# PSUM as three double and two single banks from the second batch on: a second product on two banks, attention in four pieces, double-bank relus

## The chip, the cores and the metric

One core of a Trainium2 chip runs the whole kernel. The metric is device time in microseconds (us) of one execution, as a median over runs. All runs compared here are with a granted TensorE clock of 0.999 or 1.000.

Engines are named as the profile names them: PE is TensorE, PEld its weight loads, DVE VectorE, ACT ScalarE, POOL GpSimd, SP the engine that issues stores and transposing transfers. The kernel uses PSUM, the memory that PE writes its results to, as eight banks of 128 x 512 fp32.

## The reference, cut to what matters

```python
# q, k, v: (8, 8, 1024, 64); E, F: (64, 1024); w_in: (512, 2048); w_out: (2048, 512)
k_proj = np.einsum('ks,bhsd->bhkd', E, k)
v_proj = np.einsum('ks,bhsd->bhkd', F, v)
scores = np.matmul(q, k_proj.transpose(0, 1, 3, 2)) / 8
attn = softmax(scores)                       # over the 64 projected keys
x = np.matmul(attn, v_proj) -> (8192, 512)   # heads side by side
h = np.maximum(x @ w_in, 0.0)                # first product
out = h * h @ w_out                          # second product
```

## The kernel before: the parts that matter

The kernel works batch by batch (b = 0 to 7). While PE computes the two dense products of batch b, small pieces of attention for batch b+1 are slipped in between. A batch is two chunks of 512 tokens. A chunk's first product runs in eight pairs of blocks (k = 0 to 7), each block four matmuls into one PSUM bank; ACT takes the relu out of the bank, DVE squares the pair, and from k = 4 on DVE also forms operand sums. The second product is then computed from these sums in seven products (p1 to p7 in the code) of 16 matmuls each, into 128 x 512 outputs x, y, z; one matmul fills half a bank. Where a product is cut, a and b or lo and hi are its parts.

```python
    aps = ctx.enter_context(tc.tile_pool(name="aps", bufs=2, space=bass.MemoryType.PSUM))  # 2 double banks
    fps = ctx.enter_context(tc.tile_pool(name="fps", bufs=4, space=bass.MemoryType.PSUM))  # 4 single banks
    ...
    PIECES = {       # attention of the next batch, by step of the current one (batches 2 to 6)
        1: "copy_kp", 2: "copy_vp", 4: "copy_v_down",
        20: "scores 0, scores 1, exponentials 0", 21: "exponentials 1",
        23: "sums 0, values 0 0, reciprocals 0", 25: "normalize 0 0",
        28: "scores 2, scores 3, exponentials 2", 29: "exponentials 3",
        47: "values 0 1, sums 1, reciprocals 1", 48: "normalize 0 1",
        53: "values 1 0, values 1 1", 54: "normalize 1 0", 55: "normalize 1 1",
    }
    ...
            def square(k, n, ps):                  # n: first or second block of pair k
                ...
                    nc.scalar.activation(r[:, n], ps[:], AF.Relu)
                ...                                # after n == 1: DVE squares r, then operand sums
            def step1(k, n):
                ...
                ps = ffn_psum("ps_h")              # one single bank
                first(ch, HFB * h + j, ps, range(NCB))
                square(k, n, ps)
    ...
            def p1a():                             # steps of the second product
                st["x"], st["y"], st["z"] = (bank(n) for n in ("ps_x", "ps_y", "ps_z"))
                ...
                product(st["y"], st["A11"], W11, lo, True)
            def p2a(): ...                         # x: first half of A12 * W21
            def p1b(): ...                         # y: A11 * W11, needs DVE's squares up to k = 6
            def p1c(): ...                         # y: its last two matmuls, need the square of k = 7; ACT copies y
            def p2b():
                product(st["x"], st["A12"], W21, hi)
                add(st["o0"][:, :, 0:MH], "x", st["a"])   # DVE
            ...
            second = [p1a, p2a, p1b, p1c] + lohi(p5) + lohi(p6) + lohi(p3) + lohi(p7) + [p2b]
            second += [p4_last] if last else lohi(p4)
```

Steps count through a batch: 0 to 15 the first product of the first chunk, 16 to 30 its second product, 31 to 46 and 47 to 61 the same for the second chunk. `scores`, `sums` and `values` are groups of small matmuls that use the array in several tiles at once.

The softmax here doesn't subtract the row's maximum and nothing guards it: scores larger than these inputs give would overflow.

## Time and profile before

| | kernel before |
|---|---|
| time, median of three runs | 484.09 us (483.77 to 484.11) |
| span of the profiled run | 482.4 us |
| first matmul of batch 1 | at 82.33 us |
| a steady batch (2 to 5) | 57.30 us |
| batch 6; first matmul of batch 7 to the end | 55.46; 55.8 us |

PE's share, its waits and the stretches by batch are shown in the prediction below. Beside them, two lines of the page's costliest groups: line, engine, operation, output and input, count, then busy us, mean ns of one, and idle time before.

```profile
L521 DVE TENSOR_TENSOR hsq<-h_relu 128x1024 bf16<-128x1024 f32 x123 | 149.9, 1222 | 75.0 <-ACT h_relu L513 74.2
L513 ACT ACTIVATE h_relu<-ps_h 128x512 f32<-128x512 f32 x255 | 149.4, 597 | 63.4 <-PE ps_h L459 63.0
```

These are the squares and the relus.

### The profile page before, as it was taken

How to read it: one execution, taken by the hardware profiler on the slowest of the kernel's cores; microseconds unless marked ns; L12 is line 12 of the kernel's file. 1: busy time of each engine (PE TensorE's matmuls, PEld its weight loads, DVE VectorE, ACT ScalarE, POOL GpSimd, SP SyncE). 2: the span in 40 equal slices, each digit the busy share in tenths (PEclk: the TensorE clock that was granted, in tenths of full speed). 3: DMA queues.
4: the chain of work that ended last, by engine and by line, in shares of the span. 5: the costliest groups of instructions: out<-in, count | busy, mean ns of one | idle time of the engine just before them, and what ended most of it. 6: DMA issues, size and time to landing. Idle time of an engine off the chain costs nothing.

```text
span 482.4 us, 8423 instructions
## 1 busy us (share of the span) xinstructions
PE 470.3 (97%) x3630; PEld 292.6 (61%) x3630; DVE 314.1 (65%) x382; ACT 261.5 (54%) x413; POOL 34.7 (7%) x48
## 2 busy tenths in 40 slices
PE   4899999999999999999999999999999999999997
PEld 2544676475574746657475665747557474666656
DVE  1478955554958559493776848667494855948383
ACT  2387544758427564466635667176662756545351
POOL 6540020020020001000010000100000000000000
PEclk9999999999999999999999999999999999999999
DMA  9999989579989086941859147690702102020202
GB/s 155 203 204 207 168 181 200 137 120 229 180 128 229 12 175 88 180 94 50 153 86 227 22 115 131 91 200 1 165 11 75 25 1 88 1 88 0 88 1 87
DMA packets 72789, 55.46 MB, mean 115 GB/s; under 512 B 33968, under 2 KB 64944, under 8 KB 72752
## 3 DMA queue, kind: packets, MB, share of 16 engines
q0 software_dynamic: 30624, 29.36, 39.4%
q1 hardware_dynamic: 42128, 25.56, 21.1%
q8 instruction: 28, 0.46, 0.4%
q14 instruction: 9, 0.07, 0.0%
HBM read 59.24 MB, written 16.78 MB: 158 GB/s over the span
## 4 chain that ended last, share of the span: by engine, by line
PE 92%; DVE 3%; DMA 3%; ACT 1%; POOL 1%; issue 0%; POOLq 0%
PE ps_h L459 44%; PE ps_y L479 23%; PE ps_z L479 11%; PE ps_x L479 6%; DMA V_sb<-in_v_dram 3%; PE ps_kv L180 2%; PE ps_att L221 2%; PE ps_att L206 2%; DVE hsq L521 1%; DVE s L473 1%; PE ps_v L284 0%; DVE xT L246 0%; DVE xT L351 0%; PE ps_kv L181 0%; ACT h_relu L513 0%; POOL K_sb L93 0%
## 5 line engine op out<-in xcount | busy, mean ns | idle before, releaser
L459 PE MATMUL ps_h<-xT,w_in 128*128 128x512 bf16 x1024 | 224.8, 379 | 0.2 <-DVE xT L351 0.2
L521 DVE TENSOR_TENSOR hsq<-h_relu 128x1024 bf16<-128x1024 f32 x123 | 149.9, 1222 | 75.0 <-ACT h_relu L513 74.2
L513 ACT ACTIVATE h_relu<-ps_h 128x512 f32<-128x512 f32 x255 | 149.4, 597 | 63.4 <-PE ps_h L459 63.0
L459 PEld LDWEIGHTS <-w_in 128*128 128x128 bf16 x1024 | 99.7, 98 | 117.7 <-issue 1.9
L479 PEld LDWEIGHTS <-s 128*128 128x128 bf16 x1024 | 98.5, 98 | 19.8 <-issue 8.7
L479 PEld LDWEIGHTS <-hsq 128*128 128x128 bf16 x768 | 73.8, 98 | 17.3 <-issue 3.8
L479 PE MATMUL ps_y<-T,s 128*128 128x256 bf16 x512 | 62.4, 273 | 0.0
L246 DVE TENSOR_TENSOR xT<-ps_att,rs 128x1024 bf16<-128x1024 f32 x28 | 33.4, 1215 | 17.6 <-ACT rs L236 17.0
L473 DVE TENSOR_TENSOR s<-hsq 128x1024 bf16<-128x1024 bf16 x64 | 43.5, 683 | 0.0
L591 ACT COPY o_sb<-ps_y 128x512 f32<-128x512 f32 x15 | 8.8, 586 | 53.8 <-PE ps_y L479 53.7
L213 ACT ACTIVATE expT<-ps_att 128x1024 bf16<-128x1024 f32 x28 | 27.2, 1025 | 14.0 <-PE ps_att L206 14.0
L479 PE MATMUL ps_x<-w_out,hsq 128*128 128x256 bf16 x256 | 33.2, 273 | 0.0
L479 PE MATMUL ps_y<-w_out,hsq 128*128 128x256 bf16 x256 | 33.2, 273 | 0.0
L595 DVE TENSOR_TENSOR o_sb<-ps_z,p_b 128x512 f32<-128x512 f32 x16 | 11.0, 688 | 33.8 <-issue 19.9
L479 PE MATMUL ps_y<-T,hsq 128*128 128x256 bf16 x256 | 30.9, 272 | 0.0
L479 PE MATMUL ps_z<-T,s 128*128 128x256 bf16 x256 | 30.6, 273 | 0.0
L479 PE MATMUL ps_z<-w_out,s 128*128 128x256 bf16 x256 | 30.6, 273 | 0.0
L591 ACT COPY p_b<-ps_y 128x512 f32<-128x512 f32 (+1 forms) x17 | 9.4, 556 | 25.9 <-PE ps_y L479 25.8
L81 POOL DMA_DIRECT2D Q_sb<-in_q_dram x7 | 6.1, 876 | 227.7 <-DMA qT<-Q_sb 227.2
L473 DVE TENSOR_TENSOR s<-s,hsq 128x1024 bf16<-128x1024 bf16 x32 | 21.8, 684 | 0.3
L473 DVE TENSOR_TENSOR s<-hsq,s 128x1024 bf16<-128x1024 bf16 x32 | 21.7, 682 | 0.0
L591 ACT COPY p_a<-ps_y 128x512 f32<-128x512 f32 (+1 forms) x17 | 9.4, 561 | 21.8 <-PE ps_y L479 21.6
(75 smaller groups left out, 233.0 us busy)
## 6 DMA issues: line engine op xcount, KB each, us to landing
out_dram<-o_sb SPq DMA_DIRECT2D x30, 512.0 KB, 3.8
K_sb<-in_k_dram POOLq DMA_DIRECT2D x7, 1024.0 KB, 15.3
V_sb<-in_v_dram POOLq DMA_DIRECT2D x7, 1024.0 KB, 22.4
Q_sb<-in_q_dram POOLq DMA_DIRECT2D x7, 1024.0 KB, 9.4
w_out<-in_moe_w_out_dram POOLq DMA_DIRECT2D x4, 512.0 KB, 13.2
w_in<-in_moe_w_in_dram POOLq DMA_DIRECT2D x7, 256.0 KB, 10.0
K_sb<-in_k_dram POOLq DMA_DIRECT2D x2, 512.0 KB, 8.5
out_dram<-o_sb SPq DMA_DIRECT2D x3, 256.0 KB, 2.1
```

The lines of the kernel that those rows point to most:

```text
L180: nc.tensor.matmul(ps[0:KP, :], lhsT=ET[:, i, :], rhs=kv[:, :, i, :], start=f, stop=l)
L206: nc.tensor.matmul(ps[o, bank, :], lhsT=self.kT[r, 2 * pr + j, :], start=True, stop=True, rhs=self.qT[r, NT * (2 * pr + j):NT * (2 * pr + ...
L213: nc.scalar.activation(e[:], self.ps["s", pr][:], AF.Exp, scale=SCALE)
L221: nc.tensor.matmul(ps[32 * j:32 * j + 32, a, :], lhsT=weights(o, 4 * g + j), rhs=self.exp[2 * g + j // 2][o, bank, :], start=True, stop=Tr ...
L246: nc.vector.tensor_tensor(out=self.xT[:, 2 * g + e].rearrange("p a n t -> p a (n t)"), in0=self.ps["v", g, e][:], in1=self.rs[g][:], op=AL ...
L459: nc.tensor.matmul(ps[:], lhsT=w_in_blk(cb, fb), rhs=xT[:, cb, :, 2 * ch:2 * ch + 2], start=(cb == 0), stop=(cb == NCB - 1),)
L473: nc.vector.tensor_tensor(out=s[o][:, js], in0=x, in1=y, op=op)
L479: nc.tensor.matmul(ps[tb] if len(ps) == 2 else ps[0][:, tb], lhsT=lhs[:, j, tb * P:(tb + 1) * P], rhs=rhs[:, j], start=first and n == 0 an ...
L513: nc.scalar.activation(r[:, n], ps[:], AF.Relu)
L521: multiply = lambda: nc.vector.tensor_tensor(out=o, in0=r[:], in1=r[:], op=ALU.mult)
L591: nc.scalar.copy(to[:, t], ps)
L595: nc.vector.tensor_tensor(out=to[:, t], in0=ps, in1=more[:, t], op=ALU.add)
```

## The change

Its intent is to cut what PE loses each time it changes from dense matmuls to the small ones of attention and back. Larger pieces of attention need a third double bank. It is won by giving the second product two banks instead of three (x shares the bank of z), by sending every second pair of relus through the double banks, and by reordering the second product so that the shared banks come free in time. The projection moves into an attention bank too, and from batch 2 on runs half a batch earlier.

```diff
+    aps = ctx.enter_context(psum_pool("aps", 2))
+    fps = ctx.enter_context(psum_pool("fps", 2))
+    def divide_psum(first):        # called with False after batch 0
+        mixed_stack.close()
+        mixed = mixed_stack.enter_context(psum_pool(..., 2 if first else 1))
+        turns["att"] = cycle([aps, aps] if first else [aps, aps, mixed])
+        turns["ffn"] = cycle([fps, fps, mixed, mixed] if first else [fps])
 ...
         def project(self):
-            ps = self.ps["kv"] = ffn_psum("ps_kv")
+            ps = self.ps["kv"] = att_psum([P, C], F32)
 ...
     PIECES = {                                  # batches 2 to 6
-        (as above)
+        18: "scores 0, scores 1, scores 2", 20: "exponentials 0, exponentials 1", 21: "exponentials 2",
+        23: "scores 3, exponentials 3",
+        27: "sums 0, sums 1, values 0 0, reciprocals 0", 28: "reciprocals 1", 29: "normalize 0 0",
+        49: "values 0 1, values 1 0, values 1 1", 51: "normalize 0 1", 53: "normalize 1 0",
+        55: "normalize 1 1",
     }
+    AHEAD = {23: "project", 24: "copy_kp", 25: "copy_vp", 26: "copy_v_down", 33: "transpose_q"}
+    AHEAD_1 = {33: "transpose_q", 53: "project", 54: "copy_kp", 56: "copy_vp", 59: "copy_v_down"}
     BATCH_2 = {                                 # batch 1
-        24: "scores 0, scores 1, exponentials 0", ... 27: "scores 2, scores 3, ...", ...
-        30: "sums 0, sums 1, logs 0", ... 47: "values 0 0, values 0 1", 48: "normalize 0 0, normalize 0 1",
-        53: "values 1 0, values 1 1", 54: "normalize 1 0", 55: "normalize 1 1",
+        24: "scores 0, scores 1, scores 2, exponentials 0, exponentials 1", 25: "exponentials 2",
+        28: "scores 3, sums 0, exponentials 3, logs 0", 30: "sums 1", 31: "logs 1", 33: "inverses 0",
+        36: "inverses 1", 49: "values 0 0, values 0 1, values 1 0",
+        50: "normalize 0 0, normalize 0 1", 51: "normalize 1 0",
+        53: "values 1 1", 54: "normalize 1 1",
     }
 ...
-                else:
+                elif b == 0 or k % 2:
                     nc.scalar.activation(r[:, n], ps[:], AF.Relu)
+                elif n == 1:
+                    nc.scalar.activation(r[:], st["h"][:], AF.Relu)      # both banks at once
 ...
-                ps = ffn_psum("ps_h")
+                if b == 0 or k % 2:
+                    ps = ffn_psum("ps_h")
+                else:
+                    if n == 0:
+                        st["h"] = att_psum([P, 2, TCH], F32)
+                    ps = st["h"][:, n]
 ...
-            second = [p1a, p2a, p1b, p1c] + lohi(p5) + lohi(p6) + lohi(p3) + lohi(p7) + [p2b]
+            if b:
+                second = [p1a, p2a, p1b, p1c, p2b] + lohi(p6) + lohi(p5) + lohi(p7) + lohi(p3)
+            else:
+                second = (as before)
```

p2a takes 4 matmuls instead of 8 where a piece follows it, and p2b the other 12. Two operand sums move behind p2b's addition. Left out of the cut: two copies of batch 1 that move by three to four steps, and a store that moves from p2b to p3.

## The prediction

> **What bounds the kernel now.** I read the page first: busy shares, then the chain that ended last, then who PE (TensorE) waits for, then the stretches of single batches, and last the PE, ACT and DVE timelines of one batch.
>
> ```profile
> PE 470.3 (97%) x3630; PEld 292.6 (61%) x3630; DVE 314.1 (65%) x382; ACT 261.5 (54%) x413; POOL 34.7 (7%) x48
> ...
> PE 92%; DVE 3%; DMA 3%; ACT 1%; POOL 1%; issue 0%; POOLq 0%
> ```
>
> PE is busy in 97% of the span and carries 92% of the chain. DVE and ACT have a third and almost half of their time free. The complete list of PE's own waits is this:
>
> ```profile
> PE ps_E L144 <- DVE e_bf L140: 5.0, 1, 5.0
> PE ps_E L144 <- ACT e_bf L140: 1.8, 1, 1.8
> PE ps_kT L271 <- DVE kp L265: 0.6, 2, 0.3
> PE ps_att L307 <- DVE qT L299: 0.5, 2, 0.3
> PE ps_h L459 <- DVE xT L351: 0.2, 1, 0.2
> PE ps_att L320 <- DVE vp L288: 0.2, 1, 0.2
> ```
>
> All of it (8.3 us) lies in the first 35 us, which the change doesn't touch. Cut at the first matmul of each batch from batch 1 on, the stretches are:
>
> ```profile
> 82.33:141.93 59.60, 59.52 (x450) 36.38 (x448) 38.78 (x47) 32.60 (x52) 5.26 (x6) 1.00 0.91 159
> 141.93:199.24 57.31, 57.31 (x435) 35.53 (x433) 38.62 (x45) 32.13 (x50) 2.63 (x3) 1.00 0.74 131
> 199.24:256.54 57.30, 57.30 (x435) 35.55 (x432) 38.61 (x45) 32.14 (x50) 2.62 (x3) 1.00 0.59 113
> ```
>
> The second number of a row is the stretch, the third PE's busy time: a steady batch (2 to 5) takes 57.30 us and PE has no idle time in it. Batch 6 takes 55.46 (nothing to project any more), batch 7 52.4. So only what shortens PE's own stream can pay, and the room is small. What the stream holds, from the start-to-start times of groups in the PE timeline of the batch at 256.54: 64 matmuls of the first product take 13.81 us (0.216 each), twice a batch, 27.62; 16 of the second take 1.75 (0.109 each), 224 a batch, 24.5; attention has 10 groups of concurrent small matmuls at 0.216 (2.2) and the projection, 8 times 0.216 (1.7). Sum 56.0. The other 1.3 is lost where the stream changes form:
>
> ```profile
> 272.10 1.04 PE L479 MATMUL ps_y<-w_out,hsq 128*128 128x256 bf16 x8
> 273.06 0.63 PE L206 MATMUL ps_att<-qT,kT 64*64 64x512 bf16 x8
> 273.62 1.92 PE L479 MATMUL ps_z<-T,s 128*128 128x256 bf16 x16
> ...
> 311.16 1.04 PE L479 MATMUL ps_x<-w_out,hsq 128*128 128x256 bf16 x8
> 312.10 1.91 PE L479 MATMUL ps_y<-T,hsq 128*128 128x256 bf16 x16
> ```
>
> First column is the start. Eight matmuls from 272.10 fill 0.875 us, to 272.98; the next full matmul starts at 273.62. The piece of two score groups costs 0.64 us for 2 x 0.216 = 0.43 of work: 0.21 goes into entering and leaving it. All five attention pieces of a steady batch read 0.21 to 0.23 this way. The last two lines show another loss: 0.94 instead of 0.875, because ps_y is still being added by DVE (311.36 to 312.05 in its timeline). That is 0.065 us once a batch, too short for the list of waits. It also gives the delay from the end of a read to the matmul that waited for it: 0.05 us.
>
> **What the Trainium skill says.** "TensorEngine Tiling (Array Packing)", section Tiling Modes, Key Properties, states that changing the tiling mode drains TensorE. The trace agrees: 0.22 us for each piece, whatever is in it, so fewer and larger pieces save it. "Perfetto Trace Analysis", section Optimizing Scalar/DVE Operations, puts a fixed cost of about 51 ns on each ScalarE operation that reads PSUM, and says that larger operations help if the engine is saturated. The trace agrees on the size (back to back, two single relus take 1.09 us together, two double exponentials 1.95, which puts one more 512 columns at 0.44 and the fixed part at some 0.05), but ACT is 54% busy, so the condition isn't met. The same page, section Matmuls, asks that independent groups rotate through PSUM banks, so that evacuation lies beside the next group. This change gives second-product and odd-block outputs only two single banks to rotate through.
>
> **The change, part by part** (T is the moment when the first product of a chunk ends).
>
> 1. Double-bank relus: 16 of 32 relus of a batch become 8 double ones, 8 x (2 x 0.597 - 1.025) = 1.4 us less ACT. Off the path: 0.
>
> 2. Four pieces for five, in batches 2 to 6: scores 0-2; scores 3 with the projection; both sums and one values; three values. One entry less, 5 x 0.22 = **-1.1**. Batch 1 keeps its six pieces.
>
> 3. x shares the bank of z, and the order of the products changes. Between the addition of y and the fourth product there are now 16 matmuls (1.75 us) instead of 8 (0.875): the 0.065 goes, 6 times, **-0.4**. The other reuses: y is copied (0.59) behind the 12 matmuls of p2b (1.31), which fits; z must be added before p5, with p6's 1.75 between. In the second half of a steady batch I walked DVE's queue: last square ends T+2.4, three operand sums of 0.60 T+4.2, a normalization of 1.13 T+5.35, the addition T+6.05; PE reaches p5 at about T+6.2. It fits by 0.1.
>
> 4. Two single banks: at T, y takes the bank that the first matmul group of the last pair left only 0.86 us ago. A relu starts 0.20 after its group. The double relu of the pair before starts at T-1.53 and holds ACT for 0.92, so the single relu runs from T-0.61 to T-0.01, and PE starts at T+0.05. Thirteen chunks (the last has its own banks for y): **+0.65**. The square of the last pair comes some 0.4 us later on DVE than now; where no piece lies ahead of p1c (batch 7, first half of batch 1) this may cost 0.1 or so: **+0.2**.
>
> 5. The edge of batches 0 and 1. The first block of batch 1 now writes an attention bank, the one of "values 1 0", which is free only when normalization has read it. DVE starts that at 81.52 (1.15 to the next), so the bank is free at 82.75; PE wants it at 82.33. Now that block writes a bank of its own and needs the normalized tile only later. **+0.4**.
>
> 6. Batch 1, second half: three values groups go out before p1b, and two normalizations stand ahead in DVE's queue: sums until T+4.2, normalizations until T+5.35, 6.5, 7.6. The fourth values group wants the first bank at T+5.3 (0.1 to 0.2 late), the projection, now also in an attention bank, wants the second at T+5.8 and gets it at T+6.55: 0.75. Gone is a similar wait of now, where the piece at 131.32 takes 0.82 instead of 0.56 us: -0.26. Together **+0.65**.
>
> Loads: project moves forward by 30 steps, so K and V load earlier, right after Q. At 134 to 136 us three loads of 1 MB are issued for batch 4; the DMA slices show the traffic over by about 157, and the earlier projection of batch 4 wants them at about 162. Later batches have over 10 us in hand. 0.
>
> Sum: -1.1 - 0.4 + 0.65 + 0.2 + 0.4 + 0.65 = +0.4 us, on 484.1 = 484.5. The costs rest on tight walks through DVE's and ACT's queues, and a schedule laid out this closely has probably been tuned against such waits, so I take a little off: **484.2 us**.
>
> **Rivals.**
> (a) The tight reuses of the two single banks don't fit, and PE waits in every chunk, at p1a, p6 or p5. For it: slack of 0.1 us in part 3, and 0.05 already lost in part 4. Against it: no other engine is over 65% busy. Half a microsecond in each of 14 chunks would make 490.
> (b) The waits of parts 4 to 6 don't appear, since in-order queues absorb them, and only the saving is left: 484.1 - 1.5 = 482.6. For it: the steady batches are four fifths of the span.
> (c) The early projection finds its K or V not loaded at batch 2, and PE waits some microseconds once: 487. Against it: the 5 us of slack above, and loads that land 15 to 22 us after issue.
> (d) ACT is relieved and that shortens the kernel. Against it: no wait of PE on ACT after the first 20 us.
>
> **Range and chances.** The gains are at most about 1.8 us (0.4%), and the known costs about 1.9; both are far under 2%. Between (b) and a half of (a): 482.3 to 486.8. Faster by over 2% would need 9.7 us out of a stream with 1.3 us of loss a batch, practically excluded; slower by 2% needs (a) at 0.7 us a chunk.
>
> **What would show it.** A steady batch should read 57.1 to 57.2 us, with four pieces in it and 0.94 no longer before p4. p1a should start 0.05 late at each chunk. Batch 1 should read some 60.3, with a gap before the projection in its second half, and its start some 0.4 late. ACT should be busy for some 251 us. Steady batches above 57.5 would speak for (a), and I would then be wrong about a bank that is read too late; batch 1 at or below 59.6 would show that the walk of parts 5 and 6 was wrong.

## The result, and the profile after

The changed kernel took **485.21 us** (median of six runs, 484.73 to 486.56) against 484.10 for the kernel before in the same rounds. The ratio is **1.0023**, 95% interval 1.0008 to 1.0037: the same within 2%, and slower rather than faster. Ratios here are the mean time of one kernel's fast runs over that of the other's of the same rounds, so they are not quite the ratio of the medians.

The page of the changed kernel, the lines that answer to the first two of the prediction, and then the double relus:

```profile
PE 471.2 (97%) x3630; PEld 294.4 (61%) x3630; DVE 314.6 (65%) x382; ACT 245.9 (51%) x357; POOL 34.4 (7%) x48
...
PE 94%; DVE 2%; ACT 1%; DMA 1%; issue 0%; SPq 0%; DVEq 0%
...
L533 ACT ACTIVATE h_relu<-ps_att 128x1024 f32<-128x1024 f32 x56 | 57.4, 1024 | 62.7 <-PE ps_att L477 62.7
```

ACT is busy for 15.6 us less, and the kernel isn't faster for it. PE's share of the chain has even risen. What PE waits for (from its list of waits, us in total, times, longest) has new entries:

```profile
PE ps_att L196 <- DVE xT L262: 0.7, 1, 0.7
...
PE ps_att L477 <- DVE xT L262: 0.3, 1, 0.3
...
PE ps_att L237 <- DVE xT L262: 0.2, 1, 0.2
```

In all three PE wants to write an attention bank and DVE is still reading it in a normalization (L262). L196 is the projection, L477 the first product, L237 a values group.

The stretches by batch, cut at the first matmul of each batch (the second number is the stretch), from batch 1 to the end without the repeats of batches 3 to 5:

```profile
82.92:143.59 60.67, 59.76 (x448) 36.74 (x448) 38.59 (x47) 31.78 (x46) 5.25 (x6) 1.00 0.90 158
143.59:200.74 57.15, 57.15 (x434) 35.82 (x432) 38.71 (x45) 29.73 (x42) 2.62 (x3) 1.00 0.80 148
...
372.19:427.50 55.31, 55.31 (x419) 34.96 (x417) 37.46 (x42) 29.09 (x40) 0.00 (x0) 1.00 0.11 39
427.50:483.60 56.10, 52.59 (x354) 34.08 (x351) 32.95 (x39) 22.53 (x36) 0.00 (x0) 0.99 0.16 57
```

| stretch | before | after | difference |
|---|---|---|---|
| up to the first matmul of batch 1 | 82.33 | 82.92 | +0.59 |
| batch 1 | 59.60 | 60.67 | +1.07 |
| batches 2 to 5 | 57.31, 57.30, 57.30, 57.30 | 57.15 each | -0.61 in all |
| batch 6 | 55.46 | 55.31 | -0.15 |
| batch 7 and the end | 55.77 | 56.06 | +0.29 |
| span | 482.4 | 483.6 | +1.2 |

(The last window above was cut at 483.60; the span ends at 483.56, so the table has 56.06.)

So the steady batches gained what they were to gain, and it went back in places that each occur once: the edge of batches 0 and 1, batch 1 itself, and batch 7.

One caution: the position of batch 1's first matmul moved between 81.7 and 84.5 us over the profiles. In the run at 84.5 nothing was edited before batch 2. This is a scatter of the start, and probably most of why whole times need 0.3% to tell two kernels apart. The stretches from batch 1 on repeat to 0.02 us where the edit doesn't touch them, so the experiments are read from the stretches first and from the times second.

### The profile page after: what moved, and what is told of

The parts are those of the page before. It is cut to its first block, busy times and chain, and to the rows that moved or that the text cites. A ratio compares the mean times of both kernels' runs of the same rounds, so it can differ in the third digit from the quotient of the medians.

```text
span 483.6 us, 8400 instructions
## 1 busy us (share of the span) xinstructions
PE 471.2 (97%) x3630; PEld 294.4 (61%) x3630; DVE 314.6 (65%) x382; ACT 245.9 (51%) x357; POOL 34.4 (7%) x48
## 2 busy tenths in 40 slices
DMA packets 72789, 55.46 MB, mean 115 GB/s; under 512 B 33968, under 2 KB 64944, under 8 KB 72752
## 4 chain that ended last, share of the span: by engine, by line
PE 94%; DVE 2%; ACT 1%; DMA 1%; issue 0%; SPq 0%; DVEq 0%
PE ps_h L477 25%; PE ps_y L497 21%; PE ps_att L477 20%; PE ps_z L497 17%; PE ps_att L196 3%; PE ps_att L237 2%; PE ps_att L222 2%; PE ps_att L497 1%; DVE xT L262 1%; DMA e_f<-in_F_dram 1%; PE ps_k L278 1%; PE ps_x L497 1%; PE ps_fill L377 1%; ACT expT L330 0%; DVE xT L367 0%
## 5 line engine op out<-in xcount | busy, mean ns | idle before, releaser
L477 PEld LDWEIGHTS <-w_in 128*128 128x128 bf16 x1024 | 99.7, 98 | 118.1 <-issue 2.4
L477 PE MATMUL ps_h<-xT,w_in 128*128 128x512 bf16 x576 | 135.0, 379 | 0.2 <-DVE xT L367 0.2
L477 PE MATMUL ps_att<-xT,w_in 128*128 128x512 bf16 x448 | 106.0, 379 | 0.3 <-DVE xT L262 0.3
L531 ACT ACTIVATE h_relu<-ps_h 128x512 f32<-128x512 f32 x143 | 83.6, 595 | 18.7 <-PE ps_h L477 18.6
L533 ACT ACTIVATE h_relu<-ps_att 128x1024 f32<-128x1024 f32 x56 | 57.4, 1024 | 62.7 <-PE ps_att L477 62.7
L497 PE MATMUL ps_y<-T,s 128*128 128x256 bf16 x480 | 57.6, 273 | 0.0
L262 DVE TENSOR_TENSOR xT<-ps_att,rs 128x1024 bf16<-128x1024 f32 x28 | 33.4, 1216 | 0.6 <-PE ps_att L237 0.6
L497 PE MATMUL ps_y<-w_out,hsq 128*128 128x256 bf16 x240 | 31.5, 273 | 0.0
L497 PE MATMUL ps_z<-w_out,hsq 128*128 128x256 bf16 x224 | 29.0, 273 | 0.0
L497 PE MATMUL ps_y<-T,hsq 128*128 128x256 bf16 x240 | 29.0, 273 | 0.0
L623 ACT COPY p_a<-ps_y 128x512 f32<-128x512 f32 x15 | 8.8, 587 | 31.4 <-PE ps_y L497 31.2
```

The costliest lines, as they stand in the source:

```text
L262: nc.vector.tensor_tensor(out=self.xT[:, 2 * g + e].rearrange("p a n t -> p a (n t)"), in0=self.ps["v", g, e][:], in1=self.rs[g][:], op=AL ...
L477: nc.tensor.matmul(ps[:], lhsT=w_in_blk(cb, fb), rhs=xT[:, cb, :, 2 * ch:2 * ch + 2], start=(cb == 0), stop=(cb == NCB - 1),)
L497: nc.tensor.matmul(ps[tb] if len(ps) == 2 else ps[0][:, tb], lhsT=lhs[:, j, tb * P:(tb + 1) * P], rhs=rhs[:, j], start=first and n == 0 an ...
L533: nc.scalar.activation(r[:], st["h"][:], AF.Relu)
L623: nc.scalar.copy(to[:, t], ps)
```

## The experiments

All outputs were correct. Each was timed in five rounds beside the kernel before. "Edit" is against the changed kernel.

| run | median us | ratio to the kernel before, 95% interval |
|---|---|---|
| e1_free_bank_first | 485.00 | 1.0015, 1.0003 to 1.0027 |
| e2_late_projection | 483.99 | 1.0000, 0.9985 to 1.0014 |
| e3_last_pair_single | 495.85 | 1.0241, 1.0225 to 1.0258 |
| e5_five_pieces | 486.33 | 1.0043, 1.0029 to 1.0057 |
| e3b_last_pair_two_banks | 484.79 | 0.9999, 0.9981 to 1.0017 |
| e4b_singles | 483.63 | 0.9977, 0.9956 to 0.9998 |
| e7_normalize_behind | 485.74 | 1.0009, 0.9988 to 1.0031 |
| e6_combined | 483.48 | 0.9972, 0.9953 to 0.9991 |
| e9_last_two_pairs | 483.29 | 0.9988, 0.9976 to 1.0000 |
| **e8_all_mends** | **482.19** | **0.9966, 0.9954 to 0.9978** |
| e10_all_mends_five_pieces | 483.42 | 0.9990, 0.9976 to 1.0004 |

The kernel before had medians of 484.18 (first four rows), 484.81 (next four) and 483.84 (last three) beside them. The last three ran on another chip than the first eight, and the changed kernel itself was timed only in the rounds of the result, so medians of different groups are not compared to a few tenths.

### The edge of batches 0 and 1 (e1)

```diff
-        turns["att"] = cycle([aps, aps] if first else [aps, aps, mixed])
+        turns["att"] = cycle([aps, aps] if first else [mixed, aps, aps])
```

> One edit: from batch 1 on the attention banks are handed out starting with the new pair instead of the pair that 'values 1 0' of batch 0 still holds. Theory (the edge of batches 0 and 1 costs because the first block's bank is freed by a normalization on DVE): the start-to-start time from the last eight matmuls of batch 0 to the first matmul of batch 1 falls from 1.34 us to about 0.88 and the kernel is about 0.45 us shorter than the changed kernel; every steady batch stays at 57.15. If the new pair contains the bank of y of batch 0 (copied by ACT 0.8 us after its last matmul), a gap on ACT takes its place and nothing is won. Rival (PE only waits for the normalized data, as it would with any bank): the gap stays at 1.34 or moves to the second group of matmuls, and the time doesn't change.

PE's timeline at the edge (start, us, what): first the kernel before, then the changed kernel, then this run.

```profile
81.45 1.05 PE L479 MATMUL ps_y<-T,hsq 128*128 128x256 bf16 x8
82.33 1.89 PE L459 MATMUL ps_h<-xT,w_in 128*128 128x512 bf16 x8
```

```profile
81.58 1.05 PE L497 MATMUL ps_y<-T,hsq 128*128 128x256 bf16 x8
82.92 1.02 PE L477 MATMUL ps_att<-xT,w_in 128*128 128x512 bf16 x4 [0.29 <-DVE xT L262]
```

```profile
81.46 1.05 PE L497 MATMUL ps_y<-T,hsq 128*128 128x256 bf16 x8
82.34 1.03 PE L477 MATMUL ps_att<-xT,w_in 128*128 128x512 bf16 x4
```

From start to start the eight matmuls take 0.88, 1.34 and 0.88 us. Handing out the bank that nobody holds takes away the whole 0.46, and steady batches stay at 57.15. The theory holds: the same data, another bank, no wait. In the medians it is 0.2 us, within the scatter of the start: this run's profile also waited 0.8 us for its first load of K, long before the edit acts.

### Batch 1's second half (e2)

```diff
-        50: "normalize 0 0, normalize 0 1", 51: "normalize 1 0", 53: "values 1 1", 54: "normalize 1 1",
+        50: "normalize 0 0", 52: "normalize 0 1", 54: "normalize 1 0", 57: "values 1 1", 58: "normalize 1 1",
-    AHEAD_1 = {33: "transpose_q", 53: "project", 54: "copy_kp", 56: "copy_vp", 59: "copy_v_down"}
+    AHEAD_1 = {33: "transpose_q", 57: "project", 58: "copy_kp", 59: "copy_vp", 61: "copy_v_down"}
```

> One edit: in batch 1 alone the fourth values group and the projection go four steps later, and normalizations stand behind the addition in DVE's queue. Theory (in batch 1 PE waits for attention banks behind DVE's normalizations, 0.19 and 0.72 us in the list of waits): both waits go, batch 1 falls from 60.67 to about 59.75 us, the kernel is 0.9 us shorter than the changed kernel. Rival (the projection waits for its data, or what is saved is given back at p5, p7 or the next batch's first projection): a wait of similar size appears elsewhere and batches 1 and 2 together stay at 117.8 us.

In the changed kernel the two waits stood one after the other:

```profile
131.52 1.04 PE L497 MATMUL ps_y<-T,s 128*128 128x256 bf16 x8
132.74 0.41 PE L237 MATMUL ps_att<-expT,vp 64*32 64x512 bf16 x8 [0.19 <-DVE xT L262]
133.87 0.38 PE L196 MATMUL ps_att<-K_sb,ET 128*64 128x512 bf16 x1 [0.72 <-DVE xT L262]
```

With the edit both have gone from PE's list. Batch 1's second half fell from 30.29 to 29.32 us, the batch from 60.67 to 59.69, and batch 2 stayed at 57.15. A little was given back at p5: p6 to p5 in batch 1 now takes 1.82 us instead of 1.75, as in the steady batches (e7). The time fell to that of the kernel before. The edit moves the pieces and the normalizations together, so it doesn't tell which of the two moves was needed.

### The double relus: a first try that went wrong (e3), and its mend (e3b)

```diff
-                elif b == 0 or k % 2:
+                elif b == 0 or k % 2 or k == 6:
-                    nc.scalar.activation(r[:, n], ps[:], AF.Relu)
+                    nc.scalar.activation(r[:, n], ps, AF.Relu)
```

> One edit: of the double relus only the last of each chunk (k = 6) becomes two single ones on the same double bank. Theory (the double relu ends late, so that p1a waits for the bank of the last pair, and DVE's last squares and additions come 0.4 us later, so that p1c waits where nothing lies ahead of it): p1a starts 0.03 to 0.04 us earlier in each of 13 chunks, and the p1c waits of 0.12, 0.14 and 0.19 us and the p5 wait of 0.11 us go: together about 1.0 us less than the changed kernel; steady batches 57.08, batch 1 about 60.35, from the start of batch 7 to the end of the trace about 55.8 instead of 56.1. Rival (the waits come from two banks being too few, whatever the relu): no change of more than 0.2 us.

It became 10 us slower. PE's timeline, and its wait in total, show why:

```profile
154.43 1.03 PE L477 MATMUL ps_att<-xT,w_in 128*128 128x512 bf16 x4
156.14 1.02 PE L477 MATMUL ps_att<-xT,w_in 128*128 128x512 bf16 x4 [0.69 <-ACT h_relu L531]
```

```profile
PE ps_att L477 <- ACT h_relu L531: 9.6, 14, 0.7
```

The two banks are one tile of the program. Once the first half had its own relu, PE waited with the second half until that relu had read the first: 14 times in 14 chunks. The experiment said nothing about the double relu's lateness; it showed that in this program a double-bank tile isn't emptied by halves while it is being filled. That the cause is the tracking of the whole tile is my reading of the program; the next run, with two tiles, no longer waits.

```diff
+                elif k == 6:
+                    ps = att_psum([P, TCH], F32)      # one tile for each block of the last pair
```

> Mended form of the run with the last pair in single relus: there PE stood 0.69 us before the second block of each last pair, since the two halves were one tile and its second half was written only after the first half had been read. Here the last pair (k = 6) gets two attention tiles of one bank each, so its two single relus start as each block ends. Theory (the late end of the last double relu is what makes p1a, p1c and p5 wait): p1a 0.04 earlier in 13 chunks, p5 0.085 earlier in the second half of steady batches, the p1c and p5 waits of batches 1 and 7 gone: steady batches 57.0, batch 1 about 60.3, batch 7 to the end 55.8, together 1.4 us less than the changed kernel. Rival (two single banks are too few, whatever the relu): within 0.3 us of the changed kernel.

Half right. The wait at p1a went in all chunks: first chunks of steady batches fell from 30.12 to 30.09. The first half of batch 1 fell from 30.38 to 30.10 (there ACT takes the squares of k = 3 and 5, and in the changed kernel DVE stands idle for 1.86 us before the square of k = 6, waiting for its double relu). But the second halves of steady batches stayed at 27.03, since p5 now waited 0.11 us instead of 0.08, and in batch 7 p1c still came late. So what made p5 and p1c wait was not the last double relu alone.

### Which double relus matter (e4b, e9)

```diff
-                elif k == 6:
+                elif k >= 2:          # e4b; k >= 4 in e9
```

> The run before carried on: every even pair but the first of a chunk gets two one-bank tiles and single relus, so 42 of 56 double relus are undone. Theory (ACT is off the path, so the double relus are worth nothing by themselves, and only the last one of a chunk costs): ACT's busy time rises from 246 to about 255 us, the time is that of the run with the last pair alone, within 0.3 us. Rival (the double relus relieve ACT and that is worth time): slower than that run by up to the 8 us that ACT gains.

> The last pair in two single banks had removed only the wait at p1a; with all pairs but the first in single banks the waits at p1c and p5 went too. Theory (from k = 4 on DVE has a square and an operand sum for each pair, 1.73 us for the 1.73 us that PE takes, so it cannot catch up: the double relu of k = 4 sets it 0.4 us back to the end of the chunk, that of k = 6 does so again): only these two pairs matter, so with k = 4 and 6 in single relus the stretches are those of the run with k = 2 as well: second half of a steady batch 26.92 us, second half of batch 7 26.04, the last square starts 0.87 us before the first product ends rather than 0.45. Rival (all pairs count, or ACT's load does): 26.95 or more, and batch 7's second half near 26.2.

In e4b ACT is busy for 257.1 us instead of 245.9, and the kernel is faster than the changed one: 343.15 us from the first matmul of batch 1 to that of batch 7, instead of 344.57. The double relus have no worth of their own; that ACT has less to do reaches nothing. But the expectation that it would equal e3b was wrong: second halves of steady batches fell to 26.92.

e9 shows the same 26.92 with only k = 4 and 6 undone. (What its expectation calls the second half of batch 7 is the first: 26.22 in the changed kernel, 26.04 as said. What it calls the last square is that of k = 6.) DVE's timeline in the second half of batch 2, from the square of k = 4 to that of k = 6; first the changed kernel, where the first product ends at 187.53, then e9, where it ends at 186.56:

```profile
183.60 1.23 DVE L541 TENSOR_TENSOR hsq<-h_relu 128x1024 bf16<-128x1024 f32 x1 [0.93 <-ACT h_relu L533]
184.75 0.69 DVE L491 TENSOR_TENSOR s<-hsq 128x1024 bf16<-128x1024 bf16 x1
185.35 1.22 DVE L541 TENSOR_TENSOR hsq<-h_relu 128x1024 bf16<-128x1024 f32 x1
186.49 0.69 DVE L491 TENSOR_TENSOR s<-s,hsq 128x1024 bf16<-128x1024 bf16 x1
187.09 1.22 DVE L541 TENSOR_TENSOR hsq<-h_relu 128x1024 bf16<-128x1024 f32 x1
```

```profile
182.22 1.23 DVE L541 TENSOR_TENSOR hsq<-h_relu 128x1024 bf16<-128x1024 f32 x1 [0.50 <-ACT h_relu L531]
183.36 0.69 DVE L491 TENSOR_TENSOR s<-hsq 128x1024 bf16<-128x1024 bf16 x1
183.96 1.22 DVE L541 TENSOR_TENSOR hsq<-h_relu 128x1024 bf16<-128x1024 f32 x1
185.10 0.69 DVE L491 TENSOR_TENSOR s<-s,hsq 128x1024 bf16<-128x1024 bf16 x1
185.70 1.22 DVE L541 TENSOR_TENSOR hsq<-h_relu 128x1024 bf16<-128x1024 f32 x1
```

In the changed kernel DVE waits once, for the double relu of k = 4 (0.93 before its square instead of 0.50). From there it runs without a gap, 1.74 us from square to square, and PE delivers a pair in 1.73. So the lateness of k = 4 is carried to the end of the chunk: the square of k = 6 starts 0.44 us before the first product ends, in e9 0.86. (Where the first product ends is worked out: the start of the chunk, 173.71 and 172.75, plus 64 matmuls in 13.81 us.) Undoing k = 6 alone (e3b) can't help there, since DVE is late already. Undoing k = 4 alone was not run. DVE has a third of its time free over the whole kernel, and none of it in this stretch.

The Trainium skill, "Perfetto Trace Analysis", section Optimizing Scalar/DVE Operations, also says this case in advance: where ScalarE or VectorE isn't saturated but causes bubbles on others, breaking up instructions may let work finish sooner. Here it did: 28 double relus broken up in two, 1.8 us less from the first matmul of batch 1 to the end (400.6 to 398.8).

### The wait at p5 (e7)

```diff
-        49: "values 0 1, values 1 0, values 1 1", 51: "normalize 0 1", 53: "normalize 1 0",
+        49: "values 0 1, values 1 0, values 1 1", 52: "normalize 0 1", 53: "normalize 1 0",
```

> One edit in the changed kernel: in batches 2 to 6 the first normalization of the second half is queued on DVE one step later, behind the addition of p2b instead of ahead of it. Theory (p5 starts late because the bank of z is freed by that addition, which ends at 193.71 where PE starts at 193.76): from p6 to p5 1.75 us instead of 1.83, second halves of steady batches 26.95 instead of 27.03, 0.4 us in all. Rival (the 0.08 is a fixed cost of the change from one weight matrix or bank to the other): unchanged.

The 0.08 us stands in the changed kernel between p6 and p5. First PE's timeline, then DVE's, where the addition that frees the bank of z ends at 193.03 + 0.68 = 193.71:

```profile
191.93 1.91 PE L497 MATMUL ps_y<-T,s 128*128 128x256 bf16 x16
193.76 1.91 PE L497 MATMUL ps_z<-T,s 128*128 128x256 bf16 x16
```

```profile
191.89 1.22 DVE L262 TENSOR_TENSOR xT<-ps_att,rs 128x1024 bf16<-128x1024 f32 x1
193.03 0.68 DVE L627 TENSOR_TENSOR o_sb<-ps_z,p_a 128x512 f32<-128x512 f32 x1
```

The 16 matmuls take 1.83 instead of 1.75. With the normalization behind the addition, they take 1.74 and the second halves 26.95 instead of 27.03, in each of the five batches. The time doesn't show it: 0.4 us is below the scatter, and this profile's start was the latest of all (84.53).

### The price of a piece (e5, e10), and everything together (e6, e8)

> One edit: in batches 2 to 6 the last piece of three values groups is split into two and one, so attention is in five pieces again, with the new banks. Theory (each entry of attention costs PE 0.22 us of drain whatever is in it): steady batches rise from 57.15 to 57.37, batch 6 from 55.31 to 55.53, the kernel by 1.1 us. Rival (the gain of the steady batches comes from the new order of products and the banks, not from the number of pieces): steady batches stay at 57.15.

```diff
-        49: "values 0 1, values 1 0, values 1 1", 51: "normalize 0 1", 53: "normalize 1 0",
+        49: "values 0 1, values 1 0", 51: "normalize 0 1", 52: "values 1 1", 53: "normalize 1 0",
```

A steady batch rose by 0.15 us only, to 57.30: the time of a batch before the change, but not the 57.37 expected. The split delays p6 and p5, and the wait of 0.08 at p5 vanishes into it (1.76 us from p6 to p5 in this run). e10 is the same split where that wait is mended already.

> The changed kernel with all mends at once: the unheld pair of banks first (-0.46), the late projection in batch 1 (-0.95), the last pair in two banks (-1.4), and in batch 1 scores and sums no longer in one piece, which cost one more change of tiling (-0.12). If these are separate causes they add up: 485.2 - 2.9 = 482.3 us, 0.4% below the kernel before; steady batches 57.0, batch 1 about 59.2, first matmul of batch 1 near 82.4. Rival (the mends remove the same wait, or make new ones): 483.3 or more.

> The run with all mends, with the last two pairs of each chunk in single relus instead of the last alone. Theory: the causes add up; from the first matmul of batch 1 to that of batch 7 342.4 us (kernel before 344.28, changed kernel 344.58), each steady batch 57.01, batch 1 59.2, no wait of PE in its list after 40 us, 482.6 us, 0.4% under the kernel before. Rival (the mends make new waits): not below the first run with all mends, 483.5.

> The run with all mends and, in batches 2 to 6, the piece of three values groups split into two and one. In the changed kernel this split cost only 0.15 us a batch where I expected 0.22; there PE also waited 0.085 us at p5, and a later p6 could hide that. Theory: without that wait the whole cost of an entry shows, 0.22 us a batch: second halves 27.14 instead of 26.92, 1.1 us in all. Rival (an entry for one group costs less than one for two): 0.15 again.

The combined runs put together the edits of e1 and e2, with that of e3b (in e6) or of e9 (in e8), and one more in batch 1:

```diff
-        28: "scores 3, sums 0, exponentials 3, logs 0", 30: "sums 1", 31: "logs 1", 33: "inverses 0",
+        28: "scores 3, exponentials 3", 30: "sums 0, sums 1, logs 0", 31: "logs 1", 33: "inverses 0",
```

The stretches of e8: batch 1, a steady one, and batch 7 with the end:

```profile
81.69:140.88 59.19, 59.19 (x450) 36.48 (x448) 38.56 (x47) 32.98 (x50) 5.25 (x6) 1.00 0.91 156
140.88:197.89 57.01, 57.01 (x435) 35.76 (x432) 39.10 (x47) 30.84 (x46) 2.62 (x3) 1.00 0.83 156
...
424.07:479.80 55.73, 52.24 (x354) 34.37 (x351) 32.95 (x39) 23.64 (x40) 0.00 (x0) 1.00 0.16 57
```

PE is busy through all of batch 1 (59.19 of 59.19), and its list of waits has nothing after the first 40 us. From the first matmul of batch 1 to that of batch 7 it takes 342.38 us against 344.28 before and 344.58 after the change, the expected 342.4. That doesn't make the single runs add up: in this stretch e2 alone is worth 0.99, e9 alone 1.42 and the separation of scores and sums 0.12, together 2.53, and e8 gains 2.20. The overlap lies in batch 1's second half, which falls from 30.29 to 29.32 in e2, to 29.87 in e9 and to 29.21 with both: e9 alone had removed the wait of the values group and shortened that of the projection, so a part of what e2 cures came from the late double relus. e8 is 0.34% faster than the kernel before, with an interval clear of 1 (the same within 2%). It is 3.0 us below the changed kernel by the stretches too: 2.57 from the first matmul of batch 1 to the end and 0.46 at the edge. e6, in which of the double relus only the last pair is undone, keeps the 27.03 of the steady batches, missed its expected 482.3, and lands between.

Separating scores and sums in batch 1 is worth 0.12: its first half takes 29.98 us in e6 and 30.10 in e3b. The two pieces show it: in e3b the groups scores 3, sums 0 and (apart) sums 1 take 0.34 us each, in e6 scores 3 takes 0.34 and both sums together 0.56.

In e10 the second halves rise from 26.92 to 27.14 or 27.15, which is 0.22 to 0.23 for one more piece. PE's timeline around the piece that was split off, in batch 2:

```profile
188.42 1.47 PE L497 MATMUL ps_z<-w_out,hsq 128*128 128x256 bf16 x12
189.82 0.41 PE L237 MATMUL ps_att<-expT,vp 64*32 64x512 bf16 x8
190.16 1.92 PE L497 MATMUL ps_y<-T,s 128*128 128x256 bf16 x16
```

The twelve matmuls of p2b take 1.40 us here and 1.31 in e8, where none follows, and the group of eight takes 0.34. With no wait beside it, the price of a piece shows whole, and 1.15 us of e8's lead is the four pieces.

## Why the prediction was right or wrong

The measured 485.21 us lies in the range, and it was to be the same within 2%. The bound (PE's own stream) and most places of loss were named as the runs then showed them, and the steady batches read the 57.15 that was expected. The size was off by 1.0 us, by these steps (sizes are start-to-start times of PE's groups, against the same groups without a wait):

- **Part 1, double relus off the path: right on worth, wrong on harmlessness.** ACT was freed of 15.6 us rather than 10 (56 times 2 x 0.597 - 1.024 is 9.5; the rest is mostly overlap, which counts once in busy time: each of the 56 doubles is followed by an operation that starts 0.1 before its end, 5.8 us in all), and e4b shows it is worth nothing. But "off the path: 0" missed that a double relu hands its first block over later; part 4 counted this for the last pair alone. That cost is in parts 3 and 4.
- **Part 2, -1.1 for one piece less: right.** e10 measures 0.22 to 0.23 a batch, 1.15 in five.
- **Part 3: "It fits by 0.1" was the largest mis-sized term.** p5 came 0.08 late in the second half of each of five batches, and 0.12 in the first half of batch 1: +0.52 where 0 was expected. The gain at p4 came eight times rather than six, 0.07 each, -0.57. So the part was worth -0.05 instead of -0.4. e7 shows the addition that was late. My walk had it end at T+6.05 with PE there at T+6.2; in the trace, with T at 187.53, it ends at T+6.18.
- **Part 4: +0.65 and +0.2, the sum right by luck.** p1a came 0.03 late instead of 0.05, 0.42 in all. p1c was taken as 0.1 or so in two chunks; it lost 0.12, 0.15 and 0.18 us in three (first half of batch 1, both halves of batch 7), 0.45. The two errors cancel: 0.87 for 0.85. The relu named was only half the cause: I walked back from k = 6, and the delay starts at k = 4 (e9 against e3b).
- **Part 5, +0.4: right**, 0.46 by e1.
- **Part 6, +0.65: right in place and cause, a little small.** PE's list has the two waits at 0.91, its idle time alone. From start to start the group before the values takes 1.22 instead of 0.97 and the values group 1.13 instead of 0.34 (e8 has them unhindered), 1.05 in all; the wait of before was 0.27. That is +0.78. Both waits go in e2.
- **Missing from the sum:** scores and sums in one piece of batch 1 change the tiling once more inside the piece, 0.12 (e6).
- **The sum of what was measured:** -1.15 - 0.05 + 0.87 + 0.46 + 0.78 + 0.12 = +1.03 us. By the profiles it is 1.05: 0.46 at the edge and 0.59 from there to the end (400.05 to 400.64). No larger cause is left over.
- **The final step, "I take a little off": wrong.** The sum said 484.5. Subtracting 0.3 because the layout had probably been tuned had no number behind it, and moved away from the result.
- **Two readings.** The 52.4 us given for batch 7 is about PE's busy time there (52.31); its stretch is 55.77. And the fixed part of a ScalarE operation comes out nearer 0.07 than 0.05: back to back, single relus start 0.494 us apart and double exponentials 0.92, so one more 512 columns is 0.43. The agreement with the page's figure is looser than the prediction says, and it compares two different functions. Nothing else rests on either.

Rival (a) was true in small: p1a, p1c and p5 do wait, for 0.03 to 0.18 us, not half a microsecond. Rival (b), only the saving left, is what e8 reaches once the causes are mended. Rival (c) didn't occur: no wait for a load shows at batch 2's projection, where V of batch 4 had landed at 158.92 us and was wanted at 163.99. Rival (d) is refuted by e4b.

## What to carry to other kernels

When one engine has no idle time left, a change has to be summed over every place where it reuses a buffer sooner, edges included: five gains of 0.15 us were lost again in one batch that ran a different plan. An operation merged into a larger one is not free off the critical path: it hands on its first half later, and if the next engine is locally full, that lateness travels to the end of the stage. Let a small wait prove itself by moving only what it waits for (another bank, one place in a queue), and read stretches of the trace where whole times scatter more than the effect.

## What the Trainium skill lacked or had wrong

- "TensorEngine Tiling (Array Packing)", section Key Properties (under Tiling Modes), says that changing the tiling mode drains TensorE, without a size. Here one more piece of tiled matmuls between dense ones costs 0.22 to 0.23 us on PE (e10; 0.21 to 0.23 for the five pieces of the kernel before, whatever they hold), and a piece that mixes two tilings 0.12 more (e6 against e3b).
- "Perfetto Trace Analysis", section Optimizing Scalar/DVE Operations, has both pieces of advice, to group operations when the engine is saturated and to break them up when it causes bubbles. It gives no case of what a merged operation hands on. Here DVE, at 65% of the span, has 1.74 us of work for each 1.73 us of PE in the second half of a first product, and there the 0.4 us by which a double relu is late isn't made up (e9).
